# An attention block with hashed masks and a gated feed forward: batch 0's turns reordered, the feed forward eight slots sooner, two pairs hashed as pairs, part of q's casts on ScalarE

## The chip, the cores and the metric

The kernel runs on one core of a Trainium2 chip. The time is device time in microseconds (us) of one execution. Several executions were timed; one more was profiled. An engine is named by its work or by its short name: TensorE (PE, its weight loads PEld), VectorE (DVE), ScalarE (ACT), GpSimd (POOL), SyncE (SP, which here only issues DMAs).

## The reference, cut to what matters

```python
def _attn_ref(q, k, v, proj):                       # q, k, v: 4 batches, 8 heads, 768 tokens, 64 wide
    q_bits = (np.einsum('bhsd,dk->bhsk', q, proj) > 0).astype(np.int64)      # 6 bits
    k_bits = (np.einsum('bhsd,dk->bhsk', k, proj) > 0).astype(np.int64)
    ...
    mask = q_bucket[:, :, :, None] == k_bucket[:, :, None, :]
    scores = scale * np.matmul(q, k.transpose(0, 1, 3, 2))
    scores = np.where(mask, scores, -1000000000.0)
    ...                                             # softmax over the keys
    return np.matmul(attn, v).astype(np.float32)

def _moe_ref(x, w_gate, w_val, w_out, rms_g):       # x: 3072 tokens, 512 wide; feed forward 1536 wide
    rms = np.sqrt(np.mean(x * x, axis=-1, keepdims=True) + 1e-06)
    xn = x / rms * rms_g
    g = xn @ w_gate
    silu = g * (1.0 / (1.0 + np.exp(-g)))
    val = xn @ w_val
    return (silu * val @ w_out).astype(np.float32)
```

The output of attention, with its heads side by side, is the x of the feed forward.

## The kernel before, in words

**Halves and slots.** Each batch is cut into two halves of 384 query rows, so there are eight halves, w = 0 to 7 (batch w // 2). Work on attention is cut into 192 slots: one slot is one third of the 768 keys (256 of them) for one head of one half. In slot s TensorE computes the scores of slot s + 1 (`scores`, line 312: two matmuls, 76 deep, because each operand carries 64 columns of k or q and 12 rows that encode the hash bits, so that unequal buckets get a large negative score), and ScalarE takes the Exp of them (`probs`, line 322). Score banks are two deep. When a head's three slots are done, `av` (line 334) multiplies the probabilities with v in two steps of nine matmuls, in the two slots that follow.

**The order of the heads.** `SLOTS` (lines 33 to 35) lists the slots. For batch 0 it interleaves the two halves pair of heads by pair of heads: pair 0 of half 0, pair 0 of half 1, pair 1 of half 0, and so on. So half 0 ends with slot 41 and half 1 with slot 47. From half 2 on, each half goes through its eight heads in turn, 24 slots each.

**Everything else hangs on slots.** The dictionary `plan` is written out by hand: `at(s, f, ..., rank)` puts a step at slot s. In each slot the scores of the next slot are issued first, then the steps with a rank below 3, then the Exp, then the other steps by rank. Every engine takes its instructions strictly in the order in which the program issues them; waits between engines follow from the tiles. So does each DMA queue: SP issues the loads and the DMAs that move hash bits, GpSimd issues the loads of the weights (`load_w`, `load_wo`), between its own work.

**Preparing q and k.** For batch 0 and the first two pairs of batch 1 (`BY_PE`), `keep_pair` turns one head's k or q: TensorE transposes three blocks into a bank `t_ps` (line 169), VectorE copies it to `kT` or `qT` in fp32 (line 177), and GpSimd casts two halves of that into the matmul operand `QK` (`casts`, `cast_half`, line 181). The cast of "even chunks" (par 0) is partitions 0 to 63, that of odd chunks (par 1) 64 to 127. The other pairs are turned by VectorE in 32 by 32 blocks (`turn_dve`, line 191, eight steps per pair, one per slot) and cast by GpSimd (`cast_pool`, line 199).

**Hashing.** `hash_head` (batch 0's heads) multiplies kT and qT of one head with the projection, each twice with shifted columns, so that all four blocks of bits start at a partition that an engine can copy from; the four products share a bank `d_ps` (line 207). `signs` (line 214, VectorE) makes bits of them, and three copies on VectorE (line 248) and one DMA on SP (line 246) move them to `QK`. `hash_heads` does two heads in one bank (one product for k and q of each), and moves all eight blocks by DMA on SP (line 261). `hash_pairs` does the same for the pairs turned by VectorE. In the plan, head h of batch 0 is turned at slots s and s + 1 and hashed at s + 2.

**The feed forward.** When a half's last head is done (`end`, three slots behind its last slot), `attn_out` (lines 349 to 370) adds a constant, divides, and squares; `norm` (lines 381 to 387) makes the reciprocal root on GpSimd, `scale_x` (line 392) makes `xn` in three pieces on VectorE, and `turn_x` transposes each on TensorE (line 399) and multiplies it with the weights of the norm into `xnT` on VectorE (line 400). Then come twelve steps of `gate` (line 411, tanh on ScalarE line 413) and `value` (lines 421 to 426, two VectorE instructions per step), and nine of `project` (line 435). Half w starts at slot 24 w + 54, and the plan runs for NS + 54 slots, 54 of them behind the last slot of attention.

Banks `t_ps`, `d_ps`, `m_ps`, `x_ps`, `g_ps`, `v_ps` and `y_ps` rotate through three buffers; `kT` has two buffers, `qT` four, the raw rows ten, and `QK` six.

Of the kernel before, what the change touches and what calls it, by code (L numbers as in the profile page):

```python
# [15 lines left out]
H = 8  # L16
# [13 lines left out]

SLOTS = [(w, 2 * hp + hh, p) for hp in range(H // 2) for w in range(2)
         for hh in range(2) for p in range(3)]
SLOTS += [(w, h, p) for w in range(2, 8) for h in range(H) for p in range(3)]
NS = len(SLOTS)
LAST = {(w, h): g for g, (w, h, p) in enumerate(SLOTS) if p == 2}

# [5 lines left out]
def kernel(  # L44
# [12 lines left out]
    nc = tc.nc  # L57
# [103 lines left out]
    def turn_pe(b, h, which, room=None):  # L161
        hp, hh = divmod(h, 2)
        qk_tile(b, hp)
        if hh == 0:
            t_tile(b, hp, which)
        src = raw[b, hp, which][:, hh].rearrange("p (c e) d -> p c (e d)", e=2)
        ps = bank("t_ps", [128, HALF]) if room is None else room
        for i in range(3):
            nc.tensor.transpose(ps[:, 128 * i : 128 * i + 128], src[:, i], ident)
        return ps  # L170

    def block(b, h, t):
        return QK[b, h // 2][0:64, h % 2, t * HALF : (t + 1) * HALF]

    def keep(eng, b, h, which, room=None):
        ps = turn_pe(b, h, which, room)
        (eng.copy if eng is nc.scalar else eng.tensor_copy)(t0(b, h, which), ps)  # L177
        return ps

    def cast_half(b, h, which, par):  # L180
        nc.gpsimd.tensor_copy(  # L181
            block(b, h, 2 * par + (which == "q")), t0(b, h, which)[64 * par : 64 * par + 64]
        )
# [20 lines left out]
    def hash_bank(parts):  # L204
        ps = bank("d_ps", [128, HALF])
        for t, (w, src) in enumerate(parts):
            nc.tensor.matmul(  # L207
                ps[32 * t : 32 * t + 32, :], w, src,
                start=True, stop=True, tile_position=(0, 32 * t),
            )  # L210
# [13 lines left out]
    def bits_tile(i):  # L224

        if i % 2 == 0:
            held.append(spool.tile([128, S], FP16, name="bits", bufs=3))
        return held[-1][:, (i % 2) * HALF : (i % 2 + 1) * HALF]
# [20 lines left out]

        return move  # L250

    def hash_heads(b, hp):
        ps = hash_bank(
            [(w[:, 0:32], t0(b, 2 * hp + hh, which))
             for hh in range(2) for w, which in ((pk, "k"), (pq, "q"))]
        )
        bt = bits_tile(0)
        signs(bt, ps)
        for hh, t in [(0, 0), (0, 2), (0, 1), (1, 0), (1, 2), (1, 1), (0, 3), (1, 3)]:
            p0 = 64 * hh + 32 * (t % 2) + 12 * (t // 2)  # L260
            nc.sync.dma_start(out=bit_rows(b, 2 * hp + hh, t), in_=bt[p0 : p0 + 12])

    def hash_pairs(b, hps):

# [43 lines left out]
    def scores(g):  # L308
        w, h, p = SLOTS[g]
        ps = scps.tile([128, 2, 512], FP32, name="s_ps")  # L310
        for j in range(2):
            nc.tensor.matmul(  # L312
                ps[:, j, 0:HALF], k_cols(w // 2, h, 2 * p + j), q_cols(w, h),
                start=True, stop=True,
            )
        sps[g] = ps

    def probs(g):
        w, h, p = SLOTS[g]
        if p == 0:  # L320
            psb[w, h] = ppool.tile([128, 3, 2, HALF], FP16, name="psb")
        nc.scalar.activation(  # L322
            psb[w, h][:, p], sps.pop(g)[:, :, 0:HALF], AF.Exp, scale=ESCALE,
        )
# [178 lines left out]
                in1=rows, op0=ALU.mult, op1=ALU.mult,  # L503
            )

    def keep_pair(b, hp, i, eng):

        keep(eng, b, 2 * hp + i // 2, "kq"[i % 2])

    def casts(b, hp, i):  # L510
        for par in range(2):
            cast_half(b, 2 * hp + i // 2, "kq"[i % 2], par)

    keep(nc.vector, 0, 0, "k")
    ps = keep(nc.scalar, 0, 0, "q")
    nc.scalar.copy(block(0, 0, 1), ps[0:64])
    columns_of_proj()
    keep(nc.vector, 0, 1, "k")
    keep(nc.scalar, 0, 1, "q", scps.tile([128, 2, 512], FP32, name="s_ps")[:, 0, 0:HALF])
    for i in (0, 2, 3):  # L520
        casts(0, 0, i)
    hash_head(0)((nc.vector, nc.scalar, nc.vector, nc.sync))
    bits1 = hash_head(1)
    scores(0)
# [6 lines left out]
    nc.sync.dma_start(out=gcol, in_=moe_rms_g.rearrange("(k p) -> p k", p=128))  # L531


    plan = {s: [] for s in range(NS + 54)}

    def at(s, f, *a, rank=3):
        plan[s].append((rank, len(plan[s]), lambda: f(*a)))
# [4 lines left out]
    def hash_step(h):  # L542
        hash_head(h)((nc.vector, nc.vector, nc.vector, nc.sync))

    at(2, cast_half, 0, 0, "q", 1)
    for h, s in ((2, 0), (3, 3), (4, 9), (5, 14), (6, 20), (7, 26)):
        for i in range(2):
            at(s + i, keep_pair, 0, h // 2, 2 * (h % 2) + i, nc.vector)
            at(s + 1 + i, casts, 0, h // 2, 2 * (h % 2) + i)
        at(s + 2, hash_step, h)  # L550
    for hp, s in ((1, 7), (2, 18), (3, 30)):
        at(s, v_prep, 0, hp)
    for hp in range(4):
        at(12 * hp + 6, v_mean, 0, hp, 2, range(6))
    for i, (t, src) in enumerate(((wg, moe_w_gate), (wv, moe_w_val))):
        at(4 * i, load_w, t, src, 0, 768)
        at(14 + 5 * i, load_w, t, src, 768, 1536)
        at(27 + 6 * i, load_wo, 6 * i, 6 * i + 6)

    for hp, loads, turns, sv in ((0, (9, 11, 15), (30, 31, 32, 33), 26),
                                 (1, (13, 16, 21), (35, 36, 38, 39), 32)):
        for which, s in zip("kqv", loads):
            at(s, load_rows, nc.sync, 1, hp, which)
        for i, s in enumerate(turns):
            at(s, keep_pair, 1, hp, i, nc.vector)
# [4 lines left out]


    work = {
# [6 lines left out]
    for (b, hp), (loads, s0, sh) in work.items():  # L581
        for which, s in zip("kqv", loads):
            at(s, load_rows if which == "v" else load_blocks, nc.sync, b, hp, which)
        for i in range(8):
            at(s0 + i, turn_dve, b, hp, "kq"[i // 4], i % 4, rank=5)
        for i in range(2):
            at(s0 + 4 + 4 * i, cast_pool, b, hp, "kq"[i])
        if sh:
            at(sh, hash_pairs, b, (hp,) if b == 1 else (hp - 1, hp))
        at(s0 + 11 if b == 1 else s0 + 9, v_prep, b, hp)  # L590
        if b > 1:
            at(s0 + 9, v_sum, b, hp)
            if hp % 2:
                at(48 * b + 1 + hp, v_mean, b, hp - 1, 4)
# [18 lines left out]
    for w in range(8):  # L613
        for h in range(H):
            end = LAST[w, h] + 3
            at(end - 1, av, w, h, 0, 9)
            at(end, av, w, h, 9, 18)
            if h % 2:
                at(end, o_step, w, h // 2, rank=4.5)
                if (w, h) != (0, 7):  # L620
                    at(end + 6, s_step, w, h // 2, rank=5)
        at(end + (1 if w == 0 else 12), norm, w, rank=5)
        for c in range(3):
            at(end + (2 if w == 0 else 20 + c), scale_x, w, c, rank=5)
            at(end + (5 + c if w == 0 else 23 + 2 * c), turn_x, w, c, rank=1)
        s0 = 24 * w + 54
        seen = set()
        for ft in range(NF):
            for f, s in ((g_step, s0 + 16 * ft // NF), (v_step, s0 + (32 * ft + 16) // (2 * NF))):
                at(s, f, w, ft, rank=4 if s in seen else 2)  # L630
                seen.add(s)
        for i in range(9 if w < 7 else 6):
            c, j = divmod(i, 3)
            at(s0 + 16 + i, project, w, c, 4 * j, 4 * j + 4, rank=1 if i == 8 else 3)


    for s in range(NS + 54):
        if 1 < s + 1 < NS:
            scores(s + 1)
        todo = steps(s)  # L640
        n = sum(r < 3 for r, _, _ in todo) if s < NS - 1 else 0
        for _, _, f in todo[:n]:
            f()
        if s < NS - 1:
            probs(s + 1)
        for _, _, f in todo[n:]:
            f()
# [48 lines left out]
```

## Time and profile before

| | |
|---|---|
| median of the runs | 352.69 us (352.18 to 354.48, 3 runs) |
| profiled execution | 354.56 us, its span 352.8 us |
| TensorE busy | 337.6 us, 96% of the span |
| VectorE busy | 241.9 us, 69% |
| ScalarE busy | 205.8 us, 58% |
| GpSimd busy | 150.7 us, 43% |
| mean granted TensorE clock | 0.990 |
| moved by DMA | 31.34 MB |

The span reaches from the first to the last instruction; the execution's own time is 1.8 us longer. Matmuls are pipelined and their ends are modelled, so that a busy TensorE is not one at its peak: what a group of matmuls costs is better read from the starts of the instructions around it. In lines of time order, the columns are start, duration, engine, line of the kernel, operation, output and inputs, count, and in brackets the idle time before it with what ended it. "SPq" and "POOLq" are the queues that issue DMAs. In lines of waits the numbers are the total in us, how often, and the longest.

### The profile page before, as it was taken

Reading aid. Unit: us, or ns where it says so; the run is one execution under the profiler, and the core shown is the slowest. Engines: PE = TensorE matmul, PEld = TensorE weight load, DVE = VectorE, ACT = ScalarE, POOL = GpSimd, SP = SyncE. Lnnn points to the kernel's source line nnn. Section 1 sums busy time; section 2 is a strip of 40 time slices with the busy share of each in tenths; the row PEclk is TensorE's granted clock in tenths of the full one; section 3 lists DMA queues with packets and bytes.
Section 4 is the critical chain, followed back from the end, with each engine's and each line's share of the span. In section 5 each row is a group of like instructions: output and inputs, shape, how many; then the busy total and the mean of one; then the engine's idle time right before and its main releaser. Section 6 shows DMA issues by size and latency. Waiting matters only on the chain.

```text
span 352.8 us, 7811 instructions
## 1 busy us (share of the span) xinstructions
PE 337.6 (96%) x3012; PEld 203.9 (58%) x3012; DVE 241.9 (69%) x535; ACT 205.8 (58%) x318; POOL 150.7 (43%) x226
## 2 busy tenths in 40 slices
PE   7899997799999999999999999999999999999995
PEld 6464563465565666566654666566656665555553
DVE  4786757868885788747875978556735675683860
ACT  3686775465674677567765767567766672332331
POOL 5768799334676347603756367511311042010000
PEclk9999999879999999999999999999999999999999
DMA  6999998456823290169302430110011001001002
GB/s 210 348 233 271 169 181 135 76 92 125 149 35 106 62 163 4 39 145 180 61 32 81 97 82 2 44 63 1 2 41 50 3 2 59 32 0 59 33 0 89
DMA packets 80052, 31.34 MB, mean 89 GB/s; under 512 B 65168, under 2 KB 77072, under 8 KB 80016
## 3 DMA queue, kind: packets, MB, share of 16 engines
q1 hardware_dynamic: 76032, 26.07, 31.0%
q0 software_dynamic: 3680, 4.72, 8.1%
q8 instruction: 23, 0.38, 0.4%
q10 hardware_dynamic: 304, 0.07, 0.1%
q14 instruction: 13, 0.11, 0.1%
HBM read 28.32 MB, written 6.29 MB: 98 GB/s over the span
## 4 chain that ended last, share of the span: by engine, by line
PE 74%; DVE 7%; POOL 3%; SPq 2%; DMA 1%; issue 1%; ACT 1%; DVEq 0%; ACTq 0%; POOLq 0%
PE y_ps L435 17%; PE g_ps L411 16%; PE v_ps L421 16%; PE s_ps L312 13%; PE o_ps L334 8%; PE d_ps L207 3%; SPq L121 2%; PE x_ps L399 1%; DMA kL<-in_k_dram 1%; POOL QK L181 1%; DVE ssp L374 1%; DVE otmp L349 1%; PE y_ps L653 1%; ACT psb L322 1%; DVE a L423 1%
## 5 line engine op out<-in xcount | busy, mean ns | idle before, releaser
L322 ACT ACTIVATE psb<-s_ps 128x768 f16<-128x768 f32 x192 | 150.1, 809 | 44.8 <-PE s_ps L312 43.5
L312 PE MATMUL s_ps<-QK 76*128 76x384 f16 x384 | 94.8, 329 | 3.5 <-ACT psb L322 1.1
L413 ACT ACTIVATE t<-g_ps 128x384 f32<-128x384 f32 x96 | 47.1, 490 | 57.4 <-PE g_ps L411 57.1
L423 DVE SCALAR_TENSOR_TENSOR a<-t,g_ps 128x384 f32<-128x384 f32 x96 | 52.8, 550 | 40.3 <-ACT t L413 38.0
L411 PE MATMUL g_ps<-xnT,wg 128*128 128x384 f16 x384 | 78.4, 326 | 0.8 <-DVE a L423 0.8
L421 PE MATMUL v_ps<-xnT,wv 128*128 128x384 f16 x384 | 78.0, 325 | 0.2
L358 POOL TENSOR_TENSOR x<-otmp,rcp 128x384 f32<-128x384 f32 x31 | 25.7, 828 | 103.9 <-DVE rcp L354 85.0
L435 PE MATMUL y_ps<-wo,ht 128*128 128x512 f16 x276 | 68.9, 379 | 0.1
L334 PEld LDWEIGHTS <-psb 128*128 128x128 f16 x1152 | 52.6, 98 | 23.3 <-issue 6.0
L424 DVE SCALAR_TENSOR_TENSOR ht<-a,v_ps 128x384 f16<-128x384 f32 x96 | 53.2, 554 | 10.9 <-PE v_ps L421 2.0
L334 PE MATMUL o_ps<-vl,psb 128*128 128x65 f16 x1152 | 57.4, 194 | 0.0
L411 PEld LDWEIGHTS <-wg 128*128 128x128 f16 x384 | 36.2, 97 | 25.0 <-issue 1.5
L421 PEld LDWEIGHTS <-wv 128*128 128x128 f16 x384 | 36.4, 97 | 24.7 <-issue 0.7
L312 PEld LDWEIGHTS <-QK 76*128 76x128 f16 x384 | 31.6, 98 | 18.4 <-issue 3.1
L435 PEld LDWEIGHTS <-ht 128*128 128x128 f16 x276 | 25.5, 97 | 26.4 <-issue 3.0
L442 ACT COPY ysb<-y_ps 128x512 f32<-128x512 f32 x23 | 13.5, 585 | 33.8 <-PE y_ps L435 33.5
L400 DVE TENSOR_TENSOR xnT<-x_ps,gcol 128x512 f16<-128x512 f16 x24 | 16.4, 686 | 16.3 <-PE x_ps L399 16.3
L370 POOL TENSOR_TENSOR sq<-x 128x384 f32<-128x384 f32 x31 | 25.6, 826 | 2.4
L349 DVE TENSOR_TENSOR otmp<-o_ps,cvb 128x390 f32<-128x390 f32 x32 | 17.9, 558 | 9.3 <-PE o_ps L334 9.0
L199 POOL CAST QK<-kT 64x768 f16<-64x768 f32 x20 | 16.6, 829 | 16.1 <-PE g_ps L411 10.6
L199 POOL CAST QK<-qT 64x768 f16<-64x768 f32 x20 | 16.9, 845 | 14.3 <-DVE qT L191 13.6
L207 PE MATMUL d_ps<-kT,pk 128*32 128x384 f32 x80 | 21.5, 496 | 0.9 <-DVE kT L177 0.9
(73 smaller groups left out, 281.1 us busy)
## 6 DMA issues: line engine op xcount, KB each, us to landing
vL<-in_v_dram SPq DMA_DIRECT2D x16, 384.0 KB
out_dram<-ysb SPq DMA_DIRECT2D x23, 256.0 KB
kL<-in_k_dram SPq DMA_DIRECT2D x40, 96.0 KB
qL<-in_q_dram SPq DMA_DIRECT2D x40, 96.0 KB
kL<-in_k_dram SPq DMA_DIRECT2D x5, 384.0 KB
qL<-in_q_dram SPq DMA_DIRECT2D x5, 384.0 KB
wg<-in_moe_w_gate_dram POOLq DMA_DIRECT2D x2, 768.0 KB, 10.9
wv<-in_moe_w_val_dram POOLq DMA_DIRECT2D x2, 768.0 KB, 10.1
```

The lines of the kernel that those rows point to most:

```text
L199: nc.gpsimd.tensor_copy(QK[b, hp][0:64, hh, o : o + S], T0[b, hp, which][64 * hh : 64 * hh + 64, :])
L207: nc.tensor.matmul(ps[32 * t : 32 * t + 32, :], w, src, start=True, stop=True, tile_position=(0, 32 * t),)
L312: nc.tensor.matmul(ps[:, j, 0:HALF], k_cols(w // 2, h, 2 * p + j), q_cols(w, h), start=True, stop=True,)
L322: nc.scalar.activation(psb[w, h][:, p], sps.pop(g)[:, :, 0:HALF], AF.Exp, scale=ESCALE,)
L334: nc.tensor.matmul(o[:, c, hh, 0:65], psb[w, h][:, jt // 2, jt % 2, 128 * c : 128 * c + 128], vls[b % 2][:, h, v_chunk(b, h, jt), 0:65], s ...
L358: eng.tensor_mul(xd.rearrange("p c (h d) -> p c h d", h=2), tmp[:, :, :, 0:64], r.to_broadcast([128, 3, 2, 64]),)
L411: nc.tensor.matmul(g, wg[:, kt, fs], xnT[w][:, kt], start=(kt == 0), stop=(kt == 3))
L413: nc.scalar.activation(t, g, AF.Tanh, scale=0.5)
L421: nc.tensor.matmul(vv, wv[:, kt, fs], xnT[w][:, kt], start=(kt == 0), stop=(kt == 3))
L423: nc.vector.scalar_tensor_tensor(out=a, in0=t, scalar=1.0, in1=g, op0=ALU.add, op1=ALU.mult)
L424: nc.vector.scalar_tensor_tensor(out=ht[w][:, ft], in0=a, scalar=0.5, in1=vv, op0=ALU.mult, op1=ALU.mult)
L435: nc.tensor.matmul(y, ht[w][:, ft, c * 128 : (c + 1) * 128], wo[:, ft, :], start=(ft == 0), stop=(ft == NF - 1),)
```

## The change

- `TURNS` gives batch 0's order pair by pair: half 0 and 1 alternate for pairs 0 and 1, then pairs 2 and 3 of half 0 follow in a row, then pairs 2 and 3 of half 1. Half 0 ends with slot 35 instead of 41.
- The feed forward of half w starts at slot 24 w + 46 instead of 24 w + 54, and the plan has NS + 46 slots. For half 0, `scale_x` is one slot later behind `end`; for the others `norm`, `scale_x` and `turn_x` come sooner behind `end`.
- Pairs 2 and 3 of batch 0 are hashed with `hash_heads`, a pair at once, at slots 13 and 21, in place of four `hash_head`. There, blocks 0 and 1 of each head are copied by VectorE and blocks 2 and 3 move by DMA; the order of the blocks is changed for all callers.
- The cast of q's even chunks goes from GpSimd to ScalarE, which reads the bank `t_ps` itself, for the ten q's that `keep_pair` turns.
- Preparations of batch 0's pairs 2 and 3 and of batch 1, loads of weights and of rows, and the means of v get new slots.

```diff
-SLOTS = [(w, 2 * hp + hh, p) for hp in range(H // 2) for w in range(2)
-         for hh in range(2) for p in range(3)]
+TURNS = [(0, 0), (1, 0), (0, 1), (1, 1), (0, 2), (0, 3), (1, 2), (1, 3)]
+SLOTS = [(w, 2 * hp + hh, p) for w, hp in TURNS for hh in range(2) for p in range(3)]
...
-    def keep(eng, b, h, which, room=None):
+    def keep(eng, b, h, which, room=None, direct=False):
         ps = turn_pe(b, h, which, room)
         (eng.copy if eng is nc.scalar else eng.tensor_copy)(t0(b, h, which), ps)
-        return ps
+        if direct:
+            nc.scalar.copy(block(b, h, 1), ps[0:64])
...
-    def hash_heads(b, hp):
+    def hash_heads(b, hp, eng=nc.sync):
...
-        for hh, t in [(0, 0), (0, 2), (0, 1), (1, 0), (1, 2), (1, 1), (0, 3), (1, 3)]:
+        for hh, t in [(0, 2), (1, 2), (0, 0), (0, 1), (1, 0), (1, 1), (0, 3), (1, 3)]:
             p0 = 64 * hh + 32 * (t % 2) + 12 * (t // 2)
-            nc.sync.dma_start(out=bit_rows(b, 2 * hp + hh, t), in_=bt[p0 : p0 + 12])
+            dst, src = bit_rows(b, 2 * hp + hh, t), bt[p0 : p0 + 12]
+            if t > 1 or eng is nc.sync:
+                nc.sync.dma_start(out=dst, in_=src)
+            else:
+                eng.tensor_copy(dst, src)
...
-    def keep_pair(b, hp, i, eng):
-        keep(eng, b, 2 * hp + i // 2, "kq"[i % 2])
+    def keep_pair(b, hp, i):
+        keep(nc.vector, b, 2 * hp + i // 2, "kq"[i % 2], direct=i % 2)
     def casts(b, hp, i):
-        for par in range(2):
+        for par in range(i % 2, 2):
             cast_half(b, 2 * hp + i // 2, "kq"[i % 2], par)
...
-    for i in (0, 2, 3):
-        casts(0, 0, i)
+    casts(0, 0, 0)
+    casts(0, 0, 2)
+    cast_half(0, 1, "q", 0)
...
-    at(2, cast_half, 0, 0, "q", 1)
-    for h, s in ((2, 0), (3, 3), (4, 9), (5, 14), (6, 20), (7, 26)):
-        for i in range(2):
-            at(s + i, keep_pair, 0, h // 2, 2 * (h % 2) + i, nc.vector)
-            at(s + 1 + i, casts, 0, h // 2, 2 * (h % 2) + i)
-        at(s + 2, hash_step, h)
-    for hp, s in ((1, 7), (2, 18), (3, 30)):
-        at(s, v_prep, 0, hp)
-    for hp in range(4):
-        at(12 * hp + 6, v_mean, 0, hp, 2, range(6))
+    for h in range(2):
+        at(2 + h, cast_half, 0, h, "q", 1)
+    for hp, turns, sv in ((1, (0, 1, 3, 4), 7), (2, (8, 9, 11, 12), 19), (3, (15, 17, 18, 20), 25)):
+        for i, s in enumerate(turns):
+            at(s, keep_pair, 0, hp, i)
+            at(s + 1, casts, 0, hp, i)
+        at(sv, v_prep, 0, hp)
+    at(2, hash_step, 2)
+    at(5, hash_step, 3)
+    at(13, hash_heads, 0, 2, nc.vector)
+    at(21, hash_heads, 0, 3, nc.vector)
+    for hp, s in enumerate((6, 16, 30, 36)):
+        at(s, v_mean, 0, hp, 2, range(6))
     for i, (t, src) in enumerate(((wg, moe_w_gate), (wv, moe_w_val))):
-        at(4 * i, load_w, t, src, 0, 768)
-        at(14 + 5 * i, load_w, t, src, 768, 1536)
-        at(27 + 6 * i, load_wo, 6 * i, 6 * i + 6)
-    for hp, loads, turns, sv in ((0, (9, 11, 15), (30, 31, 32, 33), 26),
-                                 (1, (13, 16, 21), (35, 36, 38, 39), 32)):
+        at(2 + 5 * i, load_w, t, src, 0, 768)
+        at(20 + 6 * i, load_w, t, src, 768, 1536)
+        at(38 + 6 * i, load_wo, 6 * i, 6 * i + 6)
+    for hp, loads, turns, sv in ((0, (10, 14, 17), (28, 30, 31, 33), 35),
+                                 (1, (16, 18, 23), (40, 41, 43, 44), 47)):
...
-        (1, 2): ((22, 25, 30), 35, 47), (1, 3): ((37, 41, 44), 50, 59),
+        (1, 2): ((28, 31, 34), 44, 53), (1, 3): ((46, 49, 51), 52, 61),
...
-        at(s0 + 11 if b == 1 else s0 + 9, v_prep, b, hp)
+        at(s0 + 9, v_prep, b, hp)
...
-        at(end + (1 if w == 0 else 12), norm, w, rank=5)
+        at(end + (1 if w == 0 else 9), norm, w, rank=5)
         for c in range(3):
-            at(end + (2 if w == 0 else 20 + c), scale_x, w, c, rank=5)
-            at(end + (5 + c if w == 0 else 23 + 2 * c), turn_x, w, c, rank=1)
-        s0 = 24 * w + 54
+            at(end + (3 if w == 0 else 12 + c), scale_x, w, c, rank=5)
+            at(end + (5 + c if w == 0 else 15 + 2 * c), turn_x, w, c, rank=1)
+        s0 = 24 * w + 46
...
-    for s in range(NS + 54):
+    for s in range(NS + 46):
```

More of the change, by code (lines that the diff above doesn't have):

```diff
@@ L504, in columns_of_proj @@
             )
-    def keep_pair(b, hp, i, eng):
-        keep(eng, b, 2 * hp + i // 2, "kq"[i % 2])
+    def keep_pair(b, hp, i):
+        keep(nc.vector, b, 2 * hp + i // 2, "kq"[i % 2], direct=i % 2)
     def casts(b, hp, i):
-        for par in range(2):
+        for par in range(i % 2, 2):
             cast_half(b, 2 * hp + i // 2, "kq"[i % 2], par)
     keep(nc.vector, 0, 0, "k")
-    ps = keep(nc.scalar, 0, 0, "q")
-    nc.scalar.copy(block(0, 0, 1), ps[0:64])
+    keep(nc.scalar, 0, 0, "q", direct=True)
     columns_of_proj()
@@ L531 @@
     nc.sync.dma_start(out=gcol, in_=moe_rms_g.rearrange("(k p) -> p k", p=128))
-    plan = {s: [] for s in range(NS + 54)}
+    plan = {s: [] for s in range(NS + 46)}
     def at(s, f, *a, rank=3):
@@ L566 @@
         for i, s in enumerate(turns):
-            at(s, keep_pair, 1, hp, i, nc.vector)
+            at(s, keep_pair, 1, hp, i)
             at(s + 1, casts, 1, hp, i)
```

## The prediction

> **What bounds the kernel now.** I read the page first, then the engines' busy time by stretches, the waits of two stretches, and the order of time at three places. Slot s is counted by the Exp of line 322: in time order the Exp of slot 6 starts at 16.50, of 36 at 48.89, of 42 at 57.81, of 54 at 72.42, of 66 at 94.05.
>
> ```profile
> span 352.8 us, 7811 instructions
> PE 337.6 (96%) x3012; PEld 203.9 (58%) x3012; DVE 241.9 (69%) x535; ACT 205.8 (58%) x318; POOL 150.7 (43%) x226
> PEclk9999999879999999999999999999999999999999
> ```
>
> TensorE is busy throughout, and its clock dips once, in slices 8 and 9. The stretches (us; busy TensorE, weight load, VectorE, ScalarE, GpSimd; clock; DMA) show where that "busy" is thin:
>
> ```profile
> 16.50:29.20 12.70, 11.96 (x146) 7.20 (x146) 9.28 (x19) 9.12 (x12) 9.52 (x16) 1.00 1.14 245
> 42.10:57.80 15.70, 13.90 (x151) 8.55 (x148) 11.29 (x27) 9.29 (x12) 14.56 (x25) 1.00 1.10 172
> 57.80:67.30 9.50, 7.04 (x81) 3.93 (x79) 6.78 (x19) 6.68 (x9) 6.54 (x10) 1.00 0.29 48
> 67.30:74.10 6.80, 6.43 (x53) 4.60 (x52) 5.17 (x12) 3.24 (x4) 3.07 (x4) 0.50 0.84 147
> 74.10:111.30 37.20, 36.45 (x342) 22.50 (x339) 29.62 (x67) 23.88 (x38) 18.63 (x25) 1.00 0.49 93
> ```
>
> From 42 to 58 GpSimd is full (14.56 of 15.70); from 58 to 67 TensorE is only 74% busy; then 6.8 us run at half clock; after 74 TensorE is 98 to 100% busy. What it waited for between 16.5 and 57.8, and (last line) from 74.1 to the end:
>
> ```profile
> PEld d_ps L207 <- DVE qT L177: 6.3, 6, 1.8
> DVE kT L191 <- POOL QK L181: 2.0, 1, 2.0
> PE g_ps L411 <- DVE a L423: 0.8, 1, 0.8
> ```
>
> So the first 74 us are set by waits around the hashes and by the chain that opens the feed forward; behind it only work counts. One hash with such a wait, and that chain:
>
> ```profile
> 32.80 0.83 PE L207 MATMUL d_ps<-kT,pk 128*32 128x384 f32 x2
> 33.38 0.55 DVE L177 COPY qT<-t_ps 128x384 f32<-128x384 f32 x1
> 33.98 0.11 PEld L207 LDWEIGHTS d_ps<-qT,pq 128*32 128x32 f32 x1 [1.04 <-DVE qT L177]
> 34.75 0.33 PEld L334 LDWEIGHTS <-psb 128*128 128x128 f16 x9 [0.63 <-issue]
> 60.17 0.56 DVE L349 TENSOR_TENSOR otmp<-o_ps,cvb 128x390 f32<-128x390 f32 x1 [1.05 <-PE o_ps L334]
> 65.29 1.83 DVE L392 TENSOR_SCALAR xn<-x,rstd 128x512 f16<-128x512 f32 x3 [1.37 <-POOL rstd L387]
> 66.38 0.40 PE L399 MATMUL x_ps<-ident,xn 128*128 128x128 f16 x4 [1.74 <-DVE xn L392]
> 73.25 1.24 PE L411 MATMUL g_ps<-xnT,wg 128*128 128x384 f16 x4
> ```
>
> The hash holds TensorE from 32.80 to 34.75, 1.96 us. The one at 16.39, whose operands were there, gave TensorE free at 17.18, 0.79 us. The first gate comes 13.1 us after batch 0's first half is done (60.17).
>
> **The sum goes by the first gate.** Behind it TensorE hardly waits, so the end moves with the time at which the gate starts plus the work left then. Before: slot 54, 73.25, and 0.4 us lost to the half clock until 74.1: 73.65. After: slot 46, with eight attention slots more left.
>
> *Rates.* A slot has two score matmuls (0.16 each, start to start) and on average six AV matmuls (9 in 0.47, so 0.053): 0.64 us. Exp follows Exp in 0.71, so a slot without preparation takes 0.71. Three transposes (37.61 to 37.94): 0.33. A v_mean: 0.35. Checked on slots 6 to 42: 36 x 0.64 + 16 x 0.33 + hashes (0.79, 1.0, four of 1.96, one of 3.84: 13.5) + 3 x 0.35 = 42.9; measured 41.3, so the count is 4% high.
>
> *Slots 6 to 38.* 32 x 0.64 = 20.5; twelve transposes 4.0; hash of head 3 0.79; the two pair hashes 1.1 each, because their q copies no longer stand behind otmp on VectorE (otmp is at slots 14 and 20, the copies at 12 and 20 ahead of it), so 0.3 wait is left; batch 1's pair 0 keeps q at slot 33 behind otmp of slot 32, so 1.96 as now; four v_means 1.4; ten plain slots at 0.71, 0.7 more. 31.5, less 4% 30.3. Two hashes fewer (four heads become two pairs) are in this, and so is GpSimd's relief: ten casts of 0.50 go, and the 3.84 us hash near slot 40, which followed GpSimd's jam (the 2.0 line above), isn't in these slots any more.
>
> *The casts on ScalarE.* Ten copies of 0.47 (line 516), six in these slots. Each reads the same t_ps as VectorE's copy. The last lines of the trace show what this does:
>
> ```profile
> 349.35 0.27 ACT L662 COPY ysb<-y_ps 128x128 f32<-128x128 f32 x1 [1.60 <-PE y_ps L653]
> 349.64 0.29 DVE L663 COPY ysb<-y_ps 128x128 f32<-128x128 f32 x1 [7.76 <-ACT ysb L662]
> ```
>
> Two reads of one y_ps bank, of different columns, and VectorE starts when ScalarE ends. So ScalarE's cast will wait for VectorE's copy, with the next Exp queued behind it and TensorE's score two slots on behind that Exp: 0.35 wait + 0.47 = 0.82 x 6 = 4.9. ScalarE's 32 Exps take 22.7; with 4.9 it is 27.6 against TensorE's 30.3, so the bounds are 0 and 4.9; I take 1.5, nearer to hidden. [...]
>
> So the Exp of slot 38 starts at 16.5 + 30.3 + 1.5 = 48.3, and its AV ends at 49.2.
>
> *Slot 38 to the gate.* From otmp to the first xn 5.1 us, as now. Then VectorE, in its program order: xn 0.6, xn 0.6, xnT 0.67, k copy 0.5, xn 0.6, xnT 0.67, q copy 0.5, otmp and rcp 0.65, a stream transpose 0.5, xnT 0.67: 6.0. With 0.2 to start: 11.3, gate at 60.5. Batch 1's pair 1 (transposes at 40 to 44, hash at 45) lies inside this; TensorE has 9 us of work there, so VectorE sets it.
>
> *Left over at the gate.* 8 x 0.64 = 5.1, the hash of (1,2) 1.42 (62.13 to 63.55), a v_mean 0.35: 6.9. Same point at 67.4, against 73.65: **-6.25**.
>
> *Moved DMAs.* The six weight loads (0.75 to 0.98 of GpSimd's queue each) go 2 to 11 slots later; gate's second half is wanted at slot 54, is issued at 20 and lands in 10.9, wo is issued at 44 and wanted at 62: covered, 0. The pair hashes issue four bit DMAs instead of two (0.75 each on SP, idle there) and save VectorE, for both pairs, four copies and two signs, 4 x 0.46 + 2 x 0.68 = 3.2. Pair 3 is hashed at 21 and first read at slot 30, some 6.8 us on; signs 1.5, issues 1.5, landing 5.2 (the score at 15.97 waited for a bits DMA issued before 10.8): 0 to 1.4 late, taken 0.4. SP after slot 45 (next part) 0 to 7.8, taken 0.8. In all -6.25 + 0.4 + 0.8 = **-5.05**. Norm, scale and turns of later halves, moved to end+9, +12 and +15, keep their place against the feed forward (8 slots earlier both); their cover is TensorE's full stretch, cost 0, and if it fails each late xn costs what it did at 66.38, up to 2 us.
>
> The profiled execution took 354.56 (span 352.8, 1.8 outside); the median shown is 352.69. The difference goes to the median: **347.6**.
>
> **Rivals.** *SP turns the sign.* Behind slot 45 SP must issue, in order, (1,1)'s eight bit DMAs, k of (1,3), k of (2,0), q of (1,3), v, q of (2,0), then (1,2)'s bits; the first waits for signs, at about 61.2. The rows of now:
>
> ```profile
> 36.50 4.78 SPq L121 DMA_DIRECT2D kL<-in_k_dram  x4
> 55.07 3.31 SPq L121 DMA_DIRECT2D kL<-in_k_dram  x4
> 65.24 2.72 SPq L121 DMA_DIRECT2D qL<-in_q_dram  x4
> ```
>
> Short prices: 61.2 + 6.0 + 3.3 + 3.3 + 2.7 + 0.6 + 2.7 + 1.6 + 2 to land = 83.4. Needed by the score of slot 60, 13 slots behind the gate at 1.80 (12 slots from 72.42 to 94.05): 83.9. Long prices (4.8, 4.8, 4.0, 4.0, landing 4.7): 91.7, 7.8 late, which eats 6.25: 354.2. It decides from a landing at about 90. For it: SP's slack there shrinks from some 5 us (those bits are issued at 73.40 to 76.57 now); against it: the long prices were met under the weight loads, which are done by then. *ScalarE's wait is exposed* (4.9, not 1.5): 351.0; for it the two-deep score banks, against it 2.7 us of slack. *The clock dips again.* It fell at 67.3 behind the hole at 64.6 to 66.4; the chain still leaves about 1.5 us of hole, now near 53 to 55, and a dip of 6.8 us in the opening stage costs up to 3.4, about 2.5 as TensorE also waits there: 350.1. For it the same chain, against it the busier neighbourhood. [...]
>
> **How the numbers follow.** Forecast 0.52, clock 0.18, ScalarE 0.16, SP 0.14. About 1% (3.5 us: below 349.2 or above 356.2) is what a measurement of this kernel can tell from no change; a slowdown of that size needs SP's long prices together with ScalarE's exposed wait (354.2 + 3.4 = 357.6), half of the SP case. Faster 0.48 (forecast) + 0.08 (clock) + 0.02 (ScalarE) = 0.58; same 0.04 + 0.10 + 0.13 + 0.07 (SP) = 0.34; slower 0.01 + 0.07 = 0.08. The range reaches from all bounded terms at their good end, and no hole (343), to ScalarE's or the clock's case with part of SP's (353.5); the forecast's own is 345 to 349.5.
>
> **What would show it.** Right: first gate at about 60 and slot 38 at 48; d_ps waits for qT near 2 us, not 6.3; line 191 not waiting for line 181; TensorE from the gate on over 97% busy. The casts are right if each starts when VectorE's copy of the bank ends. Wrong: a gate past 65, a score waiting for QK's bits near slot 60, or line 191 waiting for kL on VectorE, or TensorE at 90% behind the gate, because VectorE (now 29.6 of 37.2) can't carry feed forward and transposes together.

## The result, and the profile after

The changed kernel takes 351.46 us in the median of 20 executions (348.80 to 354.54), the kernel before 353.14 (351.84 to 355.03); the ratio is 0.9948 [0.9924, 0.9971]. It is faster, by 1.7 us, a third of the 5 us that were forecast (347.6). Ratios, here and below, leave out executions more than 1.5% above the fastest of their kernel, while medians and ranges hold all of them (one of the 20 here is left out, and five of the 12 in the row 351.87 of the table below).

The profiled execution of the changed kernel took 349.88 us, 4.7 us less than the profiled one of the kernel before (354.56). The prediction was made against that one execution, and the pair of profiles agrees with it almost exactly. The medians don't. Both halves of this have to be explained.

First the page after, the rows that answer to those of before:

```profile
span 348.1 us, 7781 instructions
PE 332.3 (95%) x2996; PEld 202.8 (58%) x2996; DVE 238.4 (68%) x529; ACT 210.8 (61%) x328; POOL 146.9 (42%) x216
PEclk9979999999999999999999999999999999999999
```

The clock's dip has moved from slices 8 and 9 to slice 3. The same stretches as before:

```profile
16.50:29.20 12.70, 12.22 (x120) 7.86 (x120) 5.80 (x15) 8.32 (x12) 6.36 (x11) 0.76 0.81 152
42.10:57.80 15.70, 12.77 (x156) 8.85 (x156) 10.25 (x27) 12.03 (x19) 10.10 (x17) 1.00 1.14 186
57.80:67.30 9.50, 7.85 (x73) 4.58 (x74) 7.56 (x16) 4.92 (x9) 5.62 (x8) 1.00 0.79 137
74.10:111.30 37.20, 36.87 (x339) 21.86 (x337) 28.98 (x66) 22.28 (x34) 20.04 (x26) 1.00 0.70 140
```

GpSimd's jam from 42 to 58 us is gone (10.10 busy instead of 14.56). But between 57.8 and 67.3, in which the first gate now lies, TensorE is still only 83% busy. The order of time at the places that the prediction named, and the first wait behind the gate:

```profile
51.09 0.56 DVE L356 TENSOR_TENSOR otmp<-o_ps,cvb 128x390 f32<-128x390 f32 x1 [1.49 <-PE o_ps L341]
54.86 0.47 ACT L180 CAST QK<-t_ps 64x384 f16<-64x384 f32 x1 [0.81 <-DVE qT L178]
55.97 0.40 PE L406 MATMUL x_ps<-ident,xn 128*128 128x128 f16 x4 [1.38 <-DVE xn L399]
61.20 0.81 PE L418 MATMUL g_ps<-xnT,wg 128*128 128x384 f16 x4 [0.55 <-DVE xnT L407]
63.98 0.48 PE L319 MATMUL s_ps<-QK 76*128 76x384 f16 x2 [1.05 <-DMA QK<-bits]
```

The gate starts at 61.20 (forecast 60.5), ScalarE's cast at 54.86 waits 0.81 us for VectorE's copy of the bank (as forecast), and at 63.98 the scores of slot 48 have waited 1.05 us for hash bits of batch 1's pair 0, which come by DMA. That wait is not in the prediction.

### The profile page after: what moved, and what is told of

The parts are those of the page before. It is cut to its first block, busy times and chain, and to the rows that moved or that the text cites. A ratio compares the mean times of both kernels' runs of the same rounds, so it can differ in the third digit from the quotient of the medians.

```text
span 348.1 us, 7781 instructions
## 1 busy us (share of the span) xinstructions
PE 332.3 (95%) x2996; PEld 202.8 (58%) x2996; DVE 238.4 (68%) x529; ACT 210.8 (61%) x328; POOL 146.9 (42%) x216
## 4 chain that ended last, share of the span: by engine, by line
PE 84%; DVE 7%; DMA 3%; ACT 3%; issue 1%; SPq 1%; POOL 0%; DVEq 0%; ACTq 0%
PE y_ps L442 17%; PE g_ps L418 17%; PE v_ps L428 17%; PE s_ps L319 15%; PE o_ps L341 8%; PE d_ps L209 4%; DMA QK<-bits 3%; PE x_ps L406 1%; PE t_ps L169 1%; ACT psb L329 1%; DVE a L430 1%; PE z_ps L487 1%; PE y_ps L664 1%; DVE otmp L356 1%; DVE bits L216 1%
## 5 line engine op out<-in xcount | busy, mean ns | idle before, releaser
L329 ACT ACTIVATE psb<-s_ps 128x768 f16<-128x768 f32 x192 | 150.2, 808 | 30.3 <-PE s_ps L319 29.1
L365 POOL TENSOR_TENSOR x<-otmp,rcp 128x384 f32<-128x384 f32 x31 | 26.4, 852 | 96.0 <-DVE rcp L361 95.4
L377 POOL TENSOR_TENSOR sq<-x 128x384 f32<-128x384 f32 x31 | 26.3, 850 | 2.4
L193 DVE STREAM_TRANSPOSE qT<-qL 128x192 f32<-128x192 f32 x40 | 20.1, 519 | 0.0
```

The lines of the kernel that those rows point to most:

```text
L329: nc.scalar.activation(psb[w, h][:, p], sps.pop(g)[:, :, 0:HALF], AF.Exp, scale=ESCALE,)
L365: eng.tensor_mul(xd.rearrange("p c (h d) -> p c h d", h=2), tmp[:, :, :, 0:64], r.to_broadcast([128, 3, 2, 64]),)
L377: nc.gpsimd.tensor_mul(sq, xd, xd)
```

## The experiments

Every row below is a kernel against the kernel before, on the same chip (ratio of the two with its 95% interval).

| kernel | median us | lowest, highest | ratio |
|---|---|---|---|
| before, again | 353.64 | 352.70, 355.07 | 1.0012 [0.9988, 1.0035] |
| after, again | 351.97 | 348.52, 353.53 | 0.9931 [0.9894, 0.9968] |
| before, holes filled | 352.54 | 352.09, 353.96 | 0.9978 [0.9955, 1.0000] |
| after, holes filled | 350.44 | 347.65, 353.81 | 0.9898 [0.9869, 0.9926] |
| after, weight loads as before | 348.65 | 347.06, 353.19 | 0.9865 [0.9821, 0.9908] |
| before, weight loads as after | 352.65 | 351.40, 353.59 | 0.9979 [0.9957, 1.0000] |
| after, casts on GpSimd | 347.49 | 346.23, 351.16 | 0.9847 [0.9799, 0.9895] |
| after, hashed by heads | 350.51 | 349.62, 351.12 | 0.9914 [0.9881, 0.9946] |
| after, row loads as before | 352.19 | 349.48, 353.37 | 0.9949 [0.9925, 0.9973] |
| the same, weight loads as before | 350.52 | 346.08, 354.13 | 0.9889 [0.9857, 0.9921] |
| the same, casts on GpSimd | 351.87 | 347.20, 353.39 | 0.9884 [0.9846, 0.9922] |
| before, new order alone | 355.92 | 352.22, 357.22 | 1.0048 [1.0016, 1.0080] |
| after, two loads left out | 350.95 | 348.06, 353.81 | 0.9919 [0.9887, 0.9951] |
| after, half the bits by engines | 347.63 | 347.35, 349.23 | 0.9846 [0.9814, 0.9877] |
| the same, weight loads as before | 345.81 | 345.44, 347.59 | 0.9797 [0.9766, 0.9827] |
| the same, holes filled | 345.50 | 345.29, 345.61 | 0.9777 [0.9751, 0.9802] |
| before, half the bits by engines | 355.15 | 354.16, 355.83 | 1.0038 [1.0012, 1.0064] |
| the fastest, casts on GpSimd | 346.27 | 345.94, 347.05 | 0.9790 [0.9754, 0.9826] |

**Is it the clock?** Both kernels unchanged, and both with small matmuls placed where TensorE stands still:

```diff
+FILL = {6: 24, 44: 24, 47: 8}      # before: {6: 24, 41: 12, 50: 28}
 def scores(g):
     ps = scps.tile([128, 2, 512], FP32, name="s_ps")
+    for _ in range(FILL.get(g, 0)):
+        nc.tensor.matmul(ps[:, 0, HALF:512], ones16, ones16, start=True, stop=True)
```

> The kernel before, unchanged: a second trace, and the granted clock of each of its executions. Theory A (where the two half-clock windows fall in the opening is a matter of chance, and it takes 1.3 to 1.7 us per 3.4 us window): the times fall into groups by the mean clock, about 351.8 at 1.000, 352.7 at 0.995 and 354.5 at 0.990; the profiled execution that the prediction was made against was in the last group, two us above the typical one. Theory B (the profiled execution was typical, and the changed kernel's was a lucky one by its DMA landings): no relation between clock and time here.

> The changed kernel, unchanged: a second trace. Theory A: times by mean clock, about 348.2 at 1.000, 349.5 at 0.995, 350.5 at 0.990. Ratio to the kernel before 0.994 to 0.996. Theory B: times spread by 4 us at the same clock, and the second trace shows the difference as a score or a VectorE transpose waiting for a DMA near slots 6, 52 or 60.

> The kernel before with 24, 12 and 28 more small matmuls (128 columns, 0.055 us each) ahead of the scores of slots 6, 41 and 50, where TensorE waits anyway; they write columns that nothing reads. Theory A: no half-clock window is left, the spread shrinks, and the median falls by 1 to 2 us against the kernel before, to 351.5. Theory B: the median stays or rises by up to 1 us, the spread stays.

> The changed kernel with 24, 24 and 8 such matmuls ahead of the scores of slots 6, 44 and 47. Theory A: no half-clock window is left, median 348 to 348.5, 4.5 us under the kernel before (ratio 0.987) and about 3.5 under the kernel before with the same filling. Theory B: the median stays near 351.5 and the spread near 4 us.

The half-clock stretch lasted 6.83 us in the trace of before (67.28 to 74.11) and in that of after (15.70 to 22.53), both with a mean granted clock of 0.990. It is counted here as two windows of 3.41 us, so that each window is 0.005 of the mean, and the granted clock of each execution tells how many it had. Median times by the number of such windows, of all 133 executions of before that were timed beside the kernels of the table, and of the 32 of the changed kernel (7 and 2 of them had three):

| half-clock windows | before (executions) | after (executions) | difference |
|---|---|---|---|
| none | 352.30 (33) | 349.63 (5) | 2.7 |
| one | 353.26 (66) | 351.05 (9) | 2.2 |
| two | 354.56 (27) | 352.30 (16) | 2.3 |

So a window costs 1.0 to 1.4 us, and the profiled execution of before (354.56, mean clock 0.990) was an ordinary one with two windows, 1.3 us above the commonest class. At the same number of windows the change is worth 2.2 to 2.7 us. The changed kernel has two windows in 16 of 32 executions and the kernel before in 27 of 133, which takes the median's gain down to 1.7. That theory holds, but it explains under 1 us of the 3.3 that are missing. The rest stands in the other column of the results: at one and the same clock the changed kernel spreads over 4 us (two windows: 349.88 to 353.88), the kernel before over 1.7 (354.06 to 355.73). Its profiled execution was the fastest of its class. Filling removed the windows of before (all 12 executions at 0.998 or more) but not those of after (8 of 12 have one), and left after's spread as it was. The trace of the filled one shows a hole that the filling does not reach: the scores of slot 48 wait 1.99 us for hash bits, until 63.72, and the clock falls at 64.16.

The second trace of the changed kernel, without any dip, shows it. Waits from 58.5 to 80 us, and SP's queue:

```profile
PE s_ps L319 <- DMA QK<-bits: 2.1, 1, 2.1
DVE kT L193 <- DMA kL<-in_k_dram: 1.1, 1, 1.1
```

```profile
37.33 9.32 SPq L121 DMA_DIRECT2D kL<-in_k_dram  x4
46.75 7.84 SPq L121 DMA_DIRECT2D qL<-in_q_dram  x4
54.69 6.20 SPq L266 DMA_DIRECT2D QK<-bits  x8
61.56 6.10 SPq L266 DMA_DIRECT2D QK<-bits  x8
68.19 5.46 SPq L121 DMA_DIRECT2D kL<-in_k_dram  x8
```

In the trace of before the loads of q and the bits of pair 0 read:

```profile
41.37 2.99 SPq L121 DMA_DIRECT2D qL<-in_q_dram  x4
48.84 6.13 SPq L261 DMA_DIRECT2D QK<-bits  x8
```

The second column is how long SP was held. The four loads of k of batch 1's pair 2 held it for 9.32 us (4.78 in the trace of before) and those of q for 7.84 (2.99 before), so that the bits of pair 0 went out at 54.69 to 60.9, 6 us later than before. The gate came at 58.23, 3 us sooner than in the first trace, and the scores of slot 48 then stood until 62.04. An opening that was 3 us faster ended 1.4 us earlier: from the gate to the end it took 288.5 us here and 286.9 in the first trace.

**Whose load is it?** Weight loads back to the slots that they had before, and the opposite on the kernel before; and two other parts of the change undone:

```diff
-        at(2 + 5 * i, load_w, t, src, 0, 768)
-        at(20 + 6 * i, load_w, t, src, 768, 1536)
-        at(38 + 6 * i, load_wo, 6 * i, 6 * i + 6)
+        at(4 * i, load_w, t, src, 0, 768)
+        at(14 + 5 * i, load_w, t, src, 768, 1536)
+        at(27 + 6 * i, load_wo, 6 * i, 6 * i + 6)
```

```diff
-        keep(nc.vector, b, 2 * hp + i // 2, "kq"[i % 2], direct=i % 2)     # casts on GpSimd
+        keep(nc.vector, b, 2 * hp + i // 2, "kq"[i % 2], direct=False)
     def casts(b, hp, i):
-        for par in range(i % 2, 2):
+        for par in range(2):
...
-    at(13, hash_heads, 0, 2, nc.vector)                                    # hashed by heads
-    at(21, hash_heads, 0, 3, nc.vector)
+    for h, s in ((4, 10), (5, 13), (6, 18), (7, 21)):
+        at(s, hash_step, h)
```

> The changed kernel with the six weight loads back at the slots that they had before (0, 4, 14, 19, 27, 33 instead of 2, 7, 20, 26, 38, 44). Theory D (what was lost is SP's queue: the weight loads on GpSimd's queue now run at 37 to 60 us and keep SP's loads and bit DMAs from moving, so that the scores of slot 48 wait for batch 1's bits): SP's issue of k of (1,2) takes 5 us instead of 8 to 9, the bits of (1,0) go out by 50 instead of 54.7, the 2 us wait of a score for bits near 61 is gone, from the first gate to the end 286.5 us instead of 288.5, and the median is 349.5 to 350, 2 us under the changed kernel. Theory C (the loss is the clock's chance windows alone): within 0.5 us of the changed kernel, about 351.7.

> The kernel before with the weight loads at the changed kernel's slots. Theory D: SP's block loads of (1,2) stretch from 4.8 and 3.0 us towards 9 and 8, the bits of batch 1's pairs go out 5 us later; these are needed only at 61 and 70 here, so it costs between 0 and 2 us: 353.5 to 355. Theory C: no change, 353.3.

> The changed kernel with q's even chunks cast by GpSimd, as before. If ScalarE's wait for VectorE's copy of the same bank costs what the prediction took (1.5 us before slot 38, up to 4.9), slot 38 comes 1.5 us sooner and the median is 350 to 351; if the casts are a gain by GpSimd's relief, GpSimd is full again near slots 40 to 45, VectorE waits for its casts, and the median is 1 to 2 us higher, 353.

> The changed kernel with pairs 2 and 3 of batch 0 hashed head by head (at slots 10, 13, 18, 21), as before. By the prediction's rates two more hashes cost 2 x 1.1 = 2.2 us of TensorE before slot 24 and the bits need 4 more VectorE copies and 4 fewer DMAs: slot 24 comes 2.2 us later. If the time at slot 48 is set by SP (theory D), 1 to 2 us of this is hidden there and the median rises by only 0 to 1 us; if not, by 2 us, to 353.7.

With the weights earlier the median falls to 348.65, more than was expected, and the wait for bits at slot 48 is gone (slot 48 at 59.99, not 63.60). The loads were not as quick as expected: k and q of pair 2 still held SP for 6.3 and 9.5 us, as two of the weight loads still ran beside them (38.3 to 53.3), and the bits went out 2 us sooner, at 52.76. The trace ends hardly earlier than the one above (346.53 against 346.74), because the next wait of the same queue stands behind it:

```profile
71.53 0.52 DVE L193 STREAM_TRANSPOSE kT<-kL 128x192 f32<-128x192 f32 x1 [2.94 <-DMA kL<-in_k_dram]
72.49 0.70 PE L209 MATMUL d_ps<-kT,pk 128*32 128x384 f32 x1 [2.14 <-DVE a L430]
```

VectorE waits 2.94 us for k of pair 3, the feed forward's instruction on VectorE is queued behind it, and TensorE stands 2.14 us for that. The clock then dips, at 72.7. This is the rival that the prediction called "SP turns the sign", one load sooner in the queue.

Late weights cost the kernel before nothing (352.65): its loads of k stretched to 6.25 us, but nobody waited for them. Hashing by heads made slot 24 3.4 us later (37.24 against 33.85) and yet not the median, 350.51: what is lost ahead of SP's wait is hidden by it, as what is gained there is swallowed. With nothing but the casts back on GpSimd the median is 347.49, as low as the forecast. For the same reason this says little about the casts: in that execution one weight load was issued 1.9 us later (48.01 instead of 46.14), k and q of pair 2 held SP for 13.6 us instead of 17.3, and the bits went out at 51.24 instead of 54.69. It is taken up again below.

**One wait or the whole queue?** Row loads back to the slots of before, then weights too, then casts too; and the new order by itself:

```diff
-        (1, 2): ((28, 31, 34), 44, 53), (1, 3): ((46, 49, 51), 52, 61),
+        (1, 2): ((22, 25, 30), 44, 53), (1, 3): ((37, 41, 44), 52, 61),
```

```diff
 # on the kernel before: TURNS, NS + 46, s0 = 24 * w + 46, norm, scale_x and turn_x as in the change
-    for hp, s in ((1, 7), (2, 18), (3, 30)):
+    for hp, s in ((1, 7), (2, 18), (3, 25)):
         at(s, v_prep, 0, hp)
-    for hp in range(4):
-        at(12 * hp + 6, v_mean, 0, hp, 2, range(6))
+    for hp, s in enumerate((6, 16, 30, 36)):
+        at(s, v_mean, 0, hp, 2, range(6))
```

> The changed kernel with the row loads of batch 1's pairs 2 and 3 back at the slots that they had before (22, 25, 30 and 37, 41, 44 instead of 28, 31, 34 and 46, 49, 51). Theory D (SP's queue sets the time from slot 48 to 56, by the bits of (1,0) and then by k of (1,3), for which VectorE's transposes at slot 52 wait with the feed forward queued behind): k of (1,3) is there when VectorE reaches it, the wait of line 193 for kL is gone, from gate to slot 56 it takes 18 us instead of 20.3, median 349 to 349.5; a score may still wait for bits at slot 48, as the loads of (1,3) now stand between the two sets of bits. Theory C (clock alone): 351.7, no change.

> The same, and the six weight loads at the slots of before. Theory D: neither a score waits for bits nor VectorE for kL between 55 and 80; gate at 57, end 287 us later; median 346.5 to 347.5, which is the 5 us that were forecast, and one of the fastest. Theory C: 351 to 352.

> The same, and q's even chunks cast by GpSimd again. If the casts on ScalarE cost (slot 38 came 0.9 us sooner without them), median 345.5 to 346.5. If GpSimd's relief is worth more once SP is out of the way, 347.5 to 348.5.

> The kernel before with the new order of the turns, the feed forward 8 slots sooner (norm, scale and turns as in the changed kernel) and the means and one cast of v where the new order needs them; hashes by heads, casts on GpSimd, all loads and preparations of q and k as before. If the order alone carries the gain: gate about 62 to 63 (GpSimd's jam and batch 1's preparation now fall in slots 35 to 45, ahead of the norm), end 287 later, median 351. If the jam is worth more than the order: gate past 65, median 353 or more.

The first three missed. In the first, the wait for k is gone as expected, but the wait for bits at slot 48 has grown instead: k and q of pair 2 held SP for 8.1 and 8.4 us again, with two loads of v among them, and pair 0's bits went out at 56.48 only (waits from 55 to 80 us):

```profile
PE s_ps L319 <- DMA QK<-bits: 4.0, 1, 4.0
```

With the weights earlier, pair 0's bits come in time, but the loads of pair 3 now stand ahead of pair 1's bits, and the scores of slot 54 wait 3.6 us for those:

```profile
68.65 6.21 SPq L266 DMA_DIRECT2D QK<-bits  x8
73.08 0.80 PE L319 MATMUL s_ps<-QK 76*128 76x384 f16 x2 [3.59 <-DMA QK<-bits]
```

So moving loads within SP's queue only exchanged one wait for the other.

The new order alone is slower than before, 355.92, and 7 of its 12 executions have four half-clock windows. Batch 1's pair 1 is then hashed at slot 40, and TensorE waits for VectorE there, 5.9 us where the whole opening of before lost 6.3 to such waits (waits from 40 to 68, in a trace of one of its faster executions, 352.97):

```profile
PEld d_ps L207 <- DVE qT L177: 5.9, 3, 3.9
```

The gate came at 65.39. The other parts of the change are needed to make the order pay.

**Take the load off.** Two loads left out altogether; half of the bits of batch 1's pairs 0 and 1 moved by engines instead of DMA; that with the earlier weights; and that with the holes filled (24 matmuls at slots 6 and 44):

```diff
+        if (b, hp) == (1, 3) and which != "v":          # two loads left out
+            at(s, reuse, b, hp, which)                  # raw[1, 3, which] = raw[1, 2, which]
+            continue
```

```diff
-        at(turns[3] + 1, hash_heads, 1, hp)
+        at(turns[3] + 1, hash_heads, 1, hp, (nc.vector, nc.gpsimd)[hp])
```

> The changed kernel without the loads of k and q of batch 1's pair 3: its transposes read the rows of pair 2 instead (so those heads' attention is computed from the wrong rows). Theory D2 (the sum of what SP has to issue and land before slot 56 sets that slot): 8 of 44 DMAs less, about 6 to 8 us of SP; slot 56 comes at 75 to 76 instead of 78.3 to 80, no wait for kL; median 348 to 349. Theory E (each wait is its own; without this load the next one takes its place): 351 to 352.

> The changed kernel with half of the bit moves of batch 1's pairs 0 and 1 (blocks 0 and 1 of each head) copied by VectorE (pair 0) and GpSimd (pair 1) instead of by DMA: 8 DMAs of 0.76 us less on SP. Theory D2: k of (1,3) is issued 5 to 6 us sooner, the bits of (1,0) no longer hold slot 48; slot 56 at 76 to 77, median 349 to 350. Theory E: 351 to 352; or 352 to 353 if the copies on VectorE delay the norm.

> The same with the six weight loads at the slots of before. Theory D2: no wait for bits or kL between 55 and 80, gate at 57, slot 56 at 75 to 76, median 346 to 347.5 (the forecast was 347.6). Theory E: 348.5 to 350, as with the weight loads alone.

> The same with 24 small matmuls ahead of the scores of slots 6 and 44 each, which write columns that nothing reads. Theory A and D2 together: no half-clock window in nearly all runs, spread below 2 us, median 345.5 to 346.5. If holes remain elsewhere (near slot 48 or 54): windows remain in half of the runs and the median is that of the kernel without the filling.

Leaving out pair 3's loads did not do it (350.95, within the changed kernel's own scatter): those loads stand behind the bits, and the bits of pair 0 still went out at 57.4, behind 17.7 us of pair 2's loads. The sum of SP's work is therefore not the measure that it was expected to be; what counts is the bits' place behind slow loads. The bits themselves settle it. With half of them copied by engines the median falls to 347.63, the spread shrinks to 1.9 us, and the interval lies clear of the changed kernel's. (That 347.63 is the 347.6 of the prediction is partly luck: the edit is not in the prediction.) SP's queue in that trace, where k and q of pair 2 still hold SP for 9.4 and 5.3 us (8.4 and 5.9 in the first trace of the changed kernel), and the stretch around the gate (59.79), with the same stretch of the second trace of the changed kernel below it:

```profile
52.60 4.43 SPq L266 DMA_DIRECT2D QK<-bits  x4
60.24 3.06 SPq L266 DMA_DIRECT2D QK<-bits  x4
63.40 7.06 SPq L121 DMA_DIRECT2D kL<-in_k_dram  x8
```

```profile
57.80:67.30 9.50, 9.30 (x92) 5.56 (x91) 7.82 (x18) 6.08 (x11) 6.56 (x10) 1.00 0.75 143
57.80:67.30 9.50, 7.00 (x69) 4.43 (x70) 6.29 (x13) 4.28 (x7) 4.02 (x6) 1.00 0.61 120
```

TensorE is busy 9.30 of 9.50 us where it was busy 7.00, and no score waits for bits behind the gate. From the gate to the end it takes 286.05 us, against 288.5 in the second trace of the changed kernel and 286.0 by the prediction (279.1 + 6.9). Of the 4 us between the medians, the wait itself is about 2: without a half-clock window the changed kernel takes 349.63 and this one 347.56 (median of four). The rest is windows, which come less often without the hole: two of its 6 executions have any, and 27 of the changed kernel's 32. With the weights earlier as well it is 345.81, and with the holes filled 345.50, six executions all at full clock and within 0.32 us: 7.6 us under the kernel before, and the fastest version here.

**Is that edit a gain of its own, and what are the casts worth?** The same edit on the kernel before, and the fastest version with the casts on GpSimd:

> The kernel before with half of the bit moves of batch 1's pairs 0 and 1 copied by VectorE (pair 0) and GpSimd (pair 1) instead of by DMA. Theory D3 (the bits' wait is made by the change: before, they land with 2 to 5 us to spare): no gain, 353 to 354, or a loss up to 1 us, as GpSimd is full from 42 to 58. If the edit is a gain of its own: 348 to 351.

> The fastest version with q's even chunks cast by GpSimd, as before. By the prediction's term for ScalarE's wait (1.5 us before slot 38, bounds 0 and 4.9) it is faster by 0.5 to 1.5 us, 344 to 345; if GpSimd's relief is worth more, slower, 346 to 348.

On the kernel before it is a loss of 0.4%: the wait for the bits is made by the change. The casts on GpSimd are not faster but 0.8 us slower (345.94 to 347.05 against 345.29 to 345.61). The two were measured on different chips and their ratios' intervals overlap, so that a gain by the casts on ScalarE isn't shown; nor is the cost of 1.5 us that the prediction took. From slot 6 to slot 38 it takes 29.8 us without them (16.81 to 46.63) and 30.2 with them (16.53 to 46.69).

## Why the prediction was wrong in its size

*What bounds the kernel* was right: behind the gate the time is TensorE's work (36.87 of 37.20 us busy from 74.10 in the first trace), and the gate's time sets the end, as long as nothing else waits behind it.

*Slots 6 to 38*: forecast 31.8 us, measured 30.6 in the trace without a dip (16.53 to 47.17). The 30.3 of work was right; the 1.5 us for ScalarE's wait was too much, and no run shows it. The wait is there (0.81 us at 54.86), but mostly hidden: in three pairs of traces with the casts on ScalarE and on GpSimd these slots differ by 0.8, 0.1 and 0.3 us.

*Slot 38 to the gate*: forecast 12.2, measured 11.1 in both traces of the changed kernel. Half of the difference is VectorE's x, 1.13 us before and 0.56 now.

*Work left at the gate*: forecast 6.9, measured 286.05 - 279.1 = 6.95 where nothing waits.

*The moved DMAs* is the step that failed. The six weight loads were put at 0, since each lands long before it is read; what runs beside them was not priced. In the changed kernel k and q of batch 1's pair 2 are loaded beside them and hold SP for 8.4 and 5.9 us in the first trace and 9.3 and 7.8 in the second, instead of 4.8 and 3.0. That the weight loads are the reason fits the times of all these traces, but no run takes them away, so that it stays argued. The bits of batch 1's pair 0, hashed at slot 34, stand behind those loads. They are not in the prediction, which counts SP's lateness from slot 45 on; in the trace of before they had some 4 us to spare. In the changed kernel slot 48 waits for them. Together with the windows at half clock this is the 4 us: 347.63 with half of the bits off the queue, 351.5 to 352.0 with them on it, in place of the 0.8 that was taken for SP.

Behind slot 45 the short prices of the prediction were met (in the second trace the loads of k of two pairs took 5.46 us together, those of q 2.65 and 2.75), and the score of slot 60 does not wait in either trace of the changed kernel. But it is not the first reader there: VectorE wants k of pair 3 at slot 52, and waits for it 1.12 us in the second trace. The prediction had named this among the signs of being wrong, without a price.

The 0.4 for the bits of batch 0's pair 3 was right in kind and too small. The score of slot 31 waits for them, 0.79 us in the first trace and 0.77 in the second, as SP's four issues took 3.14 us (33.53 to 36.67) where the sum had 1.5:

```profile
39.48 0.34 PE L319 MATMUL s_ps<-QK 76*128 76x384 f16 x1 [0.77 <-DMA QK<-bits]
```

*The profiled execution* was taken for the median and the difference carried over. It had two half-clock windows where the commonest class has one. That the changed kernel's profiled execution (349.88) came so near to the 349.5 of the sum is luck: two windows made slots 6 to 38 last 33.4 us there, and its wait for bits was short, 1.05 us. The rival "the clock dips again" had the price right (2.5 us for two windows; 1.0 to 1.4 for one) and was given 0.18; but windows are not special to the change: 27 of the changed kernel's 32 executions have at least one, and so do 100 of the 133 of before.

Of the rivals, SP's was the right mechanism, at 0.14, but at another place and with another end: the bits of pair 0 at slot 48, not those of pair 2 at slot 60; and the waits cost 4 us with their windows, not 7.8, and did not turn the sign.

## What to carry to other kernels

When a faster opening is forecast, go through every queue that feeds the stage behind it and ask when each transfer lands, not whether it lands in time now: what had 4 us to spare becomes the next wait when it leaves 6 us later and its reader comes 2 us earlier. The moved weight loads were covered themselves, but the loads of k and q that ran beside them held SP for 8.4 and 5.9 us in the first trace instead of 4.8 and 3.0, with the bits queued behind, so that a moved load has to be priced by what else is moving at its new place. And where executions fall into classes, compare class with class, and ask which one the profile shows.

## What the runs showed of the hardware that was not expected

**Small rows beside large ones.** In the second trace of the changed kernel, from 48 to 52 us, the weight load on GpSimd's queue moved 546 packets of 1024 bytes and SP's queue 335 of 128 bytes: 0.56 MB against 0.04 MB. From 52 to 56, when GpSimd's queue moved 226, SP's moved 2560. In the first trace it was 696 packets of 1024 bytes beside 768 of 128 from 52 to 56, and 69 beside 2076 from 48 to 52. Where the weight load moved most (546 and 696 packets) the counts of the two queues are of one order, while the bytes differ 13 and 7 times. What sets the shares, no run here isolates.

**The clock changes in steps of 3.41 us.** From the rise of the clock to its fall it took 61.44 us in both traces of before, 10.24 in that of after and 68.27 in that with the earlier weights: 18, 3 and 20 times 3.413. The half-clock stretch of 6.83 us in the traces of before and after is twice that. TensorE was not idle in the 3.41 us just ahead of the fall: it was busy for 1.67 us of them in the trace of before (63.87 to 67.28), 1.65 in that of after and 1.27 in that with the earlier weights. In the trace of before they hold one hole, of 1.74 us (64.65 to 66.38). The traces give no sharp limit: with half the bits by engines the clock fell after a step with 2.0 us of work, and with the row loads as before it did not after one with 1.7. In these traces the clock first rises at different times, 3.7 to 7.0 us from the start (5.84 in that of before, 5.46 in that of after). The author's estimate from these times and the steps of 3.41 us is that a hole falls into one step or across two by chance, and that the number of windows varies with that; no run shows it. Filling the holes took the windows away where no other wait was left (six of six executions at full clock).

**VectorE beside GpSimd.** The multiplication of x (line 358) took 1.12 to 1.15 us in the three traces of before in which GpSimd's casts of 768 columns ran beside most of it, 1.19 in the one trace of the changed order in which GpSimd's cast of v (also 768 columns) did, and 0.56 in all traces in which GpSimd stood still:

```profile
60.89 1.92 POOL L199 CAST QK<-qT 64x768 f16<-64x768 f32 x2
60.99 1.13 DVE L358 TENSOR_TENSOR x<-otmp,rcp 128x384 f32<-128x384 f32 x1
```

Beside casts of 384 columns it took 0.56 and 0.76, beside copies of bits 0.57. What makes the difference was not tried.
